# Two spectral transforms and two attention layers on one core: rows normalised in pairs, two more coefficient buffers, a feature-axis group run weight by weight, and a second transform that begins earlier

## The chip, the core and the metric

The kernel runs on one core of one Trainium2 chip, in one launch. The metric is the device time in microseconds (us), here the median of three runs. A core has engines that each work through their own queue of instructions in order: PE (TensorE: matrix products, with a separate unit for loading weights), DVE (VectorE), ACT (ScalarE), POOL (GpSimd), and SP (SyncE), which here issues nearly all transfers between the chip's main memory and the working memory. Products land in eight accumulator banks that DVE and ACT read out.

## What is computed

```python
x = A_x                                   # 2048 rows of 512 features
x = x + A(layernorm(x))                   # spectral layer
x = x + B(layernorm(x))                   # attention layer
x = x + A(layernorm(x))
x = x + B(layernorm(x))

A(x): a = x @ hid_re.T; b = x @ hid_im.T                # 512 x 512
      return seq_re @ a - seq_im @ b                    # 2048 x 2048
B(x): q, k, v = x @ wq, x @ wk, x @ wv                  # 32 heads of 16
      for s in range(4):                                # segments of 512 rows
          a_dot = causal softmax(qs @ ks.T / 4) @ vs
          a_mem = (phi(qs) @ M) / (phi(qs) @ z + 1e-6)
          o     = g * a_mem + (1 - g) * a_dot
          M, z  = M + phi(ks).T @ vs, z + sum(phi(ks))
      return o @ wo
```

All products of the transforms and projections are in 32-bit precision, made of three products of split operands: each operand is split into a high part and a low part, and high by high, high by low and low by high are added (`matmul3`). A "triple" below is these three matrix products.

## The kernel before

**How the work is ordered.** The program is written as generators that are resumed at numbered slots: `place(order, gen, slots)` says at which slots the next piece of a generator is written down. On PE that order is kept as written. For the other engines and for the SP queue a scheduler orders the instructions; what it makes of them stands in the fences below. On every engine the order is fixed once the program is built: an instruction that waits holds up all behind it.

**First transform** (`place_spectral`, `direct=True`). The 16 row tiles of 128 rows are loaded (`load_rows`, four buffers with the tag `xt`), normalised one by one (`normalise`: `row_stats` for mean and variance on DVE, the power of -1/2 on POOL, `layernorm` for a correction step and the scaled row `xn` on DVE) and split into `xa` (high part on ACT, low part on POOL; both on DVE for row tile 0). The sequence axis is contracted first. `read_pairs(tcn, k)` loads the raw coefficients of step k into two buffers `craw`, one for the real and one for the imaginary part (cc = 0, 1), splits them into `chi` (ACT) and `clo` (DVE), and forms on DVE the four sums of coefficients that the second transform needs, in one of two halves of a ring `sring`, from where 1 MB goes to memory (`sum`). `contract(tcn)` is the product: per k 16 triples, which use row tiles k and k + 8. There are 4 x 8 such steps. Then the feature axis: `split_u` splits the result into `us`, and `hidden(tcn)` multiplies by the feature-axis weights `wdt` into banks `y`, one row tile after the other, 8 triples each; `finish` adds the old row (`xr`) and stores it to `mid`. The slot `end` is where `hidden(0)` begins; two triples stand in a slot for tcn = 0, three in later ones.

**Attention** (`place_attention`). `prep` normalises and transposes a row tile into `xT`; `proj` makes q and k (`pqk`), `values` makes v (`pvv`). The 32 units (segment, head group, half of the group) are ten slots apart. A unit is `stack` (two loads, `stkq` and `stkk`, which share buffers with `chi` and `clo`), `natural_max` (scores in banks `nat`, row maxima by DVE at line 560, then `mparts`), `max_rows` (a transpose `mT`, whose result is copied by a transfer into `stkq`), `softmax_values` (scores `sT`, ACT's exponentials `pT`, POOL's causal masks, and the product `pv_bank`) and `output`. `natural_max` of a unit is written 17 slots ahead of its softmax. The first unit begins `LEAD` = 70 slots after `end`.

**Second transform** (`direct=False`): the coefficients and the stored sums are read in blocks (`read_block`, ring `cring`, split into `chi` and `clo`), and `product` gives groups of six products into banks `m`. It begins at slot `a2`, three slots before the slots of the first attention layer's units end.

Of the kernel before, what the change touches and what calls it, by code (L numbers as in the profile page):

```python
# [61 lines left out]
def spectral_infini_kernel(  # L62
# [29 lines left out]
    half_neg = consts.tile([P, 1], F32, name="half_neg")  # L92
# [40 lines left out]
    def row_stats(xt, mv=None):  # L133
        st = sb.tile([P, 6], F32, name="st", bufs=2)
        V.bn_stats(st, xt)
        mv = sb.tile([P, 2], F32, name="mv", bufs=3) if mv is None else mv
        V.bn_aggr(mv, st)
        ve = sb.tile([P, 1], F32, name="ve", bufs=3)
        V.tensor_scalar_add(ve, mv[:, 1:2], EPS)  # L139
        r = sb.tile([P, 1], F32, name="r", bufs=3)  # L140
        G.tensor_tensor(out=r, in0=ve, in1=half_neg, op=ALU.pow)  # L141
        return mv, ve, r

    first_row = []
# [4 lines left out]
    def layernorm(xt, mv, ve, r, rr=None):  # L149
        t = sb.tile([P, 1], F32, name="rt", bufs=2)  # L150
        V.scalar_tensor_tensor(t, r, r, ve, op0=ALU.mult, op1=ALU.mult)
        V.tensor_scalar(t, t, -0.5, 1.5, op0=ALU.mult, op1=ALU.add)  # L152
        rr = sb.tile([P, 1], F32, name="rr", bufs=2) if rr is None else rr
        V.tensor_mul(rr, r, t)
# [32 lines left out]
    def place_spectral(x_in, x_out, t0, end, ln_at, direct):  # L187
# [5 lines left out]
        def normal(i, xt, out):  # L193
            V.tensor_scalar(
                out, xt, row_mv[:, i, 0:1], row_r[:, i : i + 1], op0=ALU.subtract, op1=ALU.mult
            )

        def normalise(i):
            leads = i == 0 and direct
            xt = load_rows(x_in[i])  # L200
            yield
            with behind_first(i in (1, HALF, HALF + 1)):
                ve, r = row_stats(xt, row_mv[:, i])[1:]
            yield
            xn = layernorm(xt, row_mv[:, i], ve, r, row_r[:, i : i + 1])
            if not direct and i < HALF:
                G.tensor_tensor(
                    out=xn[:, D // 2 :], in0=xn[:, : D // 2], in1=xn[:, D // 2 :], op=ALU.subtract
                )
            xa[i] = pair("xa", "w", 16)  # L210
            lo = split(xa[i][:, 0], xa[i][:, 1], xn, lo_engine=V if leads else G, hi_engine=V if leads else A)
            if leads:
                first_row.append(lo[1])
            yield

        def add_rows(k):
            xt = [load_rows(x_in[i]) for i in (k, k + HALF)]
            yield
            e, o = [sb.tile([P, D], F32, name="xn", bufs=2) for _ in xt]
            normal(k, xt[0], e)  # L220
            normal(k + HALF, xt[1], o)
# [47 lines left out]
        def read_pairs(tcn, k):  # L269
            raw = [pair("craw", "craw", 2, F32) for _ in range(2)]  # L270
# [13 lines left out]
            if not ring:  # L284
                ring.append(sb.tile([P, 2, 4, 512], F32, name="sring", tag="xT", bufs=1))
            t = ring[0][:, k % 2]
            (r0, r1), (i0, i1) = ([raw[cc][:, h] for h in range(2)] for cc in range(2))
            for j, p, q in (0, r0, i0), (1, i0, i1), (2, t[:, 0], i1), (3, t[:, 2], r1):
                V.tensor_tensor(out=t[:, j], in0=p, in1=q, op=ALU.add)
# [91 lines left out]
        for i in range(NT):  # L381
            t = ln_at(i)
            place(3, normalise(i), [t, t, t] if i == 0 and direct else [t - 8, t - 3, t])
# [675 lines left out]
```

## Time and profile before

| | |
|---|---|
| runs | 1930.12, 1926.91, 1924.51 us; median 1926.91 us |
| the profiled execution's own time | 1924.58 us |
| its span in the trace | 1922.9 us |
| PE busy | 1811.9 us (94%) |
| DVE, ACT, POOL busy | 1325.3, 1058.9, 523.2 us |
| read from and written to main memory | 192.95 and 100.66 MB |

The profile is of one execution. A row of a timeline gives start, duration, engine, line, operation and the tiles (out<-in); in brackets is the idle time before it and what ended that. A table of stretches gives the busy time of each engine in each, the clock that TensorE was granted (1.00 is full), the share of time in which the transfer engines were busy, and GB/s.

### The profile page before, as it was taken

To read this page: it belongs to the slowest core of one execution; us is meant where nothing else is said; L and a number is where in the kernel's file an instruction comes from. 1 tells how busy PE (TensorE), PEld (TensorE's weight loads), DVE (VectorE), ACT (ScalarE), POOL (GpSimd) and SP (SyncE) were. 2 spreads that over 40 slices of the span, in tenths; PEclk is the share of its full clock that TensorE was granted. 3 is DMA by queue.
4 is the path that set the end of the run, shared out by engine and by line. 5 is a ranking of instruction groups with operands and counts; after the bars stand their busy time and mean duration, and the time that the engine had idled before them with its cause. 6 is when DMAs were issued, how large, how long until landed. Compare 5 with 4: busy or idle time off the path is not lost. (4 is left out here: it accounts for less than half of the span.)

```text
span 1922.9 us, 32039 instructions
## 1 busy us (share of the span) xinstructions
PE 1811.9 (94%) x10336; PEld 1302.1 (68%) x10336; DVE 1325.3 (69%) x4164; ACT 1058.9 (55%) x2292; POOL 523.2 (27%) x862
## 2 busy tenths in 40 slices
PE   6899999999889999999879999999989999999998
PEld 5688888788546656665448888877865566666654
DVE  7744546544877887867857687676567778777674
ACT  2221213313578777777664455443327877777775
POOL 4300000001444344546431000000044434444442
PEclk9999999999999999999989999999999999999999
DMA  6565555545434433433436677553464434344331
GB/s 217 178 203 191 181 200 188 182 143 180 153 114 143 130 120 114 147 120 120 146 100 209 212 239 238 188 180 110 165 197 127 128 96 148 115 131 141 109 122 45
DMA packets 165657, 296.51 MB, mean 154 GB/s; under 512 B 17776, under 2 KB 66928, under 8 KB 165488
## 3 DMA queue, kind: packets, MB, share of 16 engines
q1 hardware_dynamic: 162224, 293.68, 46.5%
q8 instruction: 81, 1.33, 0.3%
q10 hardware_dynamic: 3264, 0.79, 0.2%
q14 instruction: 88, 0.72, 0.1%
HBM read 192.95 MB, written 100.66 MB: 153 GB/s over the span
## 5 line engine op out<-in xcount | busy, mean ns | idle before, releaser
L560 DVE CUSTOM_DVE_ANT_0 junk<-nat,mask 128x512 bf16<-128x512 f32 (+3 forms) x1024 | 495.8, 484 | 168.1 <-PE nat L87 149.3
L626 ACT ACTIVATE pT<-sT 128x512 f32<-128x512 f32 x640 | 369.7, 599 | 15.4 <-ACT sT L625 3.4
L87 PE MATMUL u<-chi,xa 128*128 128x512 f32 x1024 | 320.4, 394 | 13.2 <-DVE xa L97 12.2
L629 POOL TENSOR_SCALAR_AFFINE_SELECT pT<-pT 128x256 f32<-128x256 f32 (+1 forms) x448 | 198.5, 457 | 411.4 <-ACT pT L626 345.9
L87 PE MATMUL nat<-stkk,stkq 96*128 96x512 bf16 (+3 forms) x1024 | 247.0, 303 | 20.7 <-DVE mx L560 15.6
L87 PE MATMUL sT<-stkq,stkk 99*128 99x256 bf16 (+3 forms) x1024 | 248.9, 306 | 13.4 <-DVE mx L560 6.8
L141 POOL TENSOR_TENSOR r<-ve,half_neg 128x1 f32<-128x1 f32 x64 | 38.5, 605 | 755.2 <-DVE ve L139 752.6
L625 ACT ACTIVATE sT<-sT 128x256 f32<-128x256 f32 (+1 forms) x640 | 207.8, 335 | 47.5 <-PE sT L87 40.4
L87 PEld LDWEIGHTS u<-chi,xa 128*128 128x128 f32 x1024 | 195.1, 191 | 54.7 <-issue 12.1
L87 PE MATMUL u<-clo,xa 128*128 128x512 f32 x512 | 202.3, 395 | 11.3 <-DVE clo L101 8.9
L99 ACT ACTIVATE chi<-craw 128x1024 fp32r<-128x1024 f32 (+1 forms) x66 | 68.2, 1034 | 225.6 <-DMA craw<-in_ct 133.3
L87 PE MATMUL y<-wdt,us 128*128 128x512 f32 x768 | 181.8, 391 | 3.3 <-DVE wdt L101 2.2
L87 PEld LDWEIGHTS <-stkk 99*128 99x128 bf16 x1024 | 82.5, 99 | 139.8 <-issue 121.0
L87 PE MATMUL pv_bank<-pT,vt 128*17 128x128 f32 (+3 forms) x2048 | 165.3, 450 | 9.7 <-POOL pT L629 9.7
L87 PEld LDWEIGHTS y<-wdt,us 128*128 128x128 f32 x768 | 143.3, 188 | 34.3 <-DVE wdt L101 3.3
L101 DVE TENSOR_TENSOR clo<-craw,chi 128x1024 fp32r<-128x1024 f32 (+1 forms) x66 | 79.5, 1206 | 103.8 <-ACT chi L99 103.6
L87 PEld LDWEIGHTS <-stkq 96*128 96x128 bf16 x1024 | 94.9, 99 | 74.6 <-issue 34.9
L87 PE MATMUL po<-wo,oh 128*128 128x512 f32 x384 | 126.8, 446 | 8.0 <-DVE rt L152 2.7
L87 PE MATMUL pqk<-xT,wq 128*128 128x512 f32 x384 | 132.0, 453 | 0.7 <-DVE mx L560 0.5
L87 PEld LDWEIGHTS pv_bank<-pT,vt 128*17 128x17 f32 x2048 | 59.6, 99 | 103.9 <-issue 79.6
L87 PE MATMUL pvv<-wv,xT 128*128 128x512 f32 x384 | 127.6, 445 | 1.6 <-DVE mx L560 1.6
L87 PE MATMUL pqk<-xT,wk 128*128 128x512 f32 x384 | 124.7, 434 | 0.0
(135 smaller groups left out, 3064.9 us busy)
## 6 DMA issues: line engine op xcount, KB each, us to landing
sum<-sring SPq DMA_DIRECT2D x32, 1024.0 KB
cring<-sum SPq DMA_DIRECT2D x128, 256.0 KB
craw<-in_ct SPq DMA_DIRECT2D x62, 512.0 KB
stkq<-scrq SPq DMA_DIRECT2D x64, 384.0 KB
stkk<-scrk SPq DMA_DIRECT2D x64, 384.0 KB
cring<-in_ct SPq DMA_DIRECT2D x96, 256.0 KB
xt<-mid SPq DMA_DIRECT2D x64, 256.0 KB
mid<-xo SPq DMA_DIRECT2D x48, 256.0 KB
```

Of the source, the lines that this page charges most:

```text
L87: return tc.keep_in_program_order(op(*args, **kwargs))
L99: A.activation(hi, src, AF.Copy, scale=scale)
L101: lo_engine.tensor_tensor(out=lo, in0=src, in1=hi.bitcast(F32), op=ALU.subtract)
L141: G.tensor_tensor(out=r, in0=ve, in1=half_neg, op=ALU.pow)
L560: V.tensor_tensor_reduce(junk[:, :n], src, mask[:, 512 - n :], 1.0, 3e38, ALU.add, ALU.min, dst,)
L625: A.activation(blocks, blocks, AF.Relu)
L626: A.activation(dst, ps, AF.Exp, scale=-SCALE)
L629: G.affine_select(blocks, blocks, pattern=[[0, n] for n in blocks.shape[1:-1]] + [[1, P]], compare_op=ALU.is_ge, fill=0.0, base=0, channel ...
```

## The change

- Rows are normalised two at a time: statistics of both, then one addition, one power and one correction (now four DVE operations in place of three) on 128x2 values, then both scaled rows. In the first transform the pairs are rows k and k + 8 (row 0 and row 8 stay single); in the second, neighbours, at other slots than before; in attention, neighbours.
- Raw coefficients of odd k go into the first half of the ring; its other half is left for the sums. So there are four raw buffers in place of two and one buffer for the sums in place of two.
- The set-up of masks and gates moves from slot 60 to 200, behind the sums of (1, 0).
- In both transforms the last feature-axis group (tcn = 3) is run weight by weight over its four row tiles at once (`hidden_last`: eight groups of 12 products, two slots apart, four banks `y` held from first to last). Its second half of `us` takes buffers of another tag. `LEAD` falls from 70 to 64.
- The first two feature-axis weights are loaded at `end` - 7 in both transforms.
- The second transform begins seven slots earlier, at LB - 10 in place of LB - 3 (LB is the number of slots of a layer's units).

```diff
+    def row_stats(xts, mv):
+        n = len(xts)
+        for j, xt in enumerate(xts):
+            st = sb.tile([P, 6], F32, name="st", bufs=2)
+            V.bn_stats(st, xt)
+            V.bn_aggr(mv[:, j], st)
+        ve = sb.tile([P, 2], F32, name="ve", bufs=3)[:, :n]
+        V.tensor_scalar_add(ve, mv[:, :, 1], EPS)
+        r = sb.tile([P, 2], F32, name="r", bufs=3)[:, :n]
+        G.tensor_tensor(out=r, in0=ve, in1=half_neg[:, :n], op=ALU.pow)
+        return ve, r
+
+    def row_scale(rr, ve, r):
+        t = sb.tile([P, 2], F32, name="rt", bufs=2)[:, : rr.shape[1]]
+        V.tensor_tensor(out=t, in0=r, in1=r, op=ALU.mult)
+        V.tensor_tensor(out=t, in0=t, in1=ve, op=ALU.mult)
+        V.tensor_scalar(t, t, -0.5, 1.5, op0=ALU.mult, op1=ALU.add)
+        V.tensor_mul(rr, r, t)
...
         def read_pairs(tcn, k):
-            raw = [pair("craw", "craw", 2, F32) for _ in range(2)]
+            if not ring:
+                ring.append(sb.tile([P, 8, 512], F32, name="sring", tag="xT", bufs=1))
+            if k % 2 == 0:
+                raw = [pair("craw", "craw", 2, F32) for _ in range(2)]
+            else:
+                raw = [ring[0][:, 0:2], ring[0][:, 2:4]]
...
-            t = ring[0][:, k % 2]
+            t = ring[0][:, 4:]
...
-                us[tcn, tt, cc] = t = pair("us", "w", 16)
+                home = ("ut", 8) if (tcn, cc) == (TC - 1, 1) else ("w", 16)
+                us[tcn, tt, cc] = t = pair("us", *home)
...
+        def hidden_last(tcn):
+            ps = [bank("y") for _ in range(LT)]
+            xr = []
+            order = list(range(2, 2 * DT)) + [0, 1]
+            for k in order:
+                cc, d = k // DT, k % DT
+                if k == order[-3]:
+                    xr = [load_rows(x_in[tcn * LT + tt], "xr") for tt in range(LT)]
+                for tt in range(LT):
+                    ut = us[tcn, tt, cc]
+                    matmul3(
+                        ps[tt],
+                        lambda h: ut[:, h, d * P : (d + 1) * P],
+                        lambda h: wdt[cc, d][:, h, :],
+                        k == order[0],
+                        k == order[-1],
+                    )
+                if k != order[-1]:
+                    yield
+            for tt in range(LT):
+                finish(ps[tt], xr[tt], x_out, tcn * LT + tt)
+            yield
...
-                    place(3, read_pairs(tcn, k), [t + 8 * k - 10, t + 8 * k - 4, t + 8 * k - 1])
+                    place(3, read_pairs(tcn, k), [t + 8 * k - 12, t + 8 * k - 4, t + 8 * k + 3])
...
-            t = end - 1 + k if direct and k < 2 else end - 12 + 2 * k if k < 2 else end - 3 + (k - 2) // 2
+            t = end - 7 + k if k < 2 else end - 3 + (k - 2) // 2
...
+            else:
+                at = run_from(end + nh // 2 + 2 * nh // 3 + 1, 2 * DT, 2)
...
-    LB, LEAD = NSEG * NG * (HG // HU) * 10, 70
+    LB, LEAD = NSEG * NG * (HG // HU) * 10, 64
...
-    a2 = b1 + LB - 3
+    a2 = b1 + LB - 10
```

**Place 1, DVE at the start of the program.** `row_mv`, `rt`, `row_r` and `xn` belong to row tile 0, `sring` and `craw` to the sums of step 0. Before:

```order
L135 BN_STATS st<-xt 128x6
L137 BN_AGGR row_mv<-st 128x2
L139 TENSOR_SCALAR ve<-row_mv 128x1
L289 TENSOR_TENSOR sring<-craw 128x512 x2
L289 TENSOR_TENSOR sring<-sring,craw 128x512
L151 SCALAR_TENSOR_TENSOR rt<-r,ve 128x1
L289 TENSOR_TENSOR sring<-sring,craw 128x512
L152 TENSOR_SCALAR rt<-rt 128x1
L154 TENSOR_TENSOR row_r<-r,rt 128x1
L156 TENSOR_SCALAR xn<-xt,row_mv,row_r 128x512
```

The same place now:

```order
L137 BN_STATS st<-xt 128x6
L138 BN_AGGR row_mv<-st 128x2
L140 TENSOR_SCALAR ve<-row_mv 128x1
L147 TENSOR_TENSOR rt<-r 128x1
L148 TENSOR_TENSOR rt<-rt,ve 128x1
L149 TENSOR_SCALAR rt<-rt 128x1
L150 TENSOR_TENSOR row_r<-r,rt 128x1
L159 TENSOR_SCALAR xn<-xt,row_mv,row_r 128x512
L97 CAST xa<-xn 128x512
L97 TENSOR_TENSOR xa<-xn,xa 128x512
```

The four sums of step 0 have gone behind the four low parts `clo` of that step. On SP the load of row tile 8 now stands behind the four coefficient loads of step 0, and no longer ahead of them. Further on in the first transform DVE's row of the sums of step k + 1 stands between the two `clo` of step k; before, the two `clo` stood together between two rows of sums.

**Place 2, PE around the first scores of the first unit** (`nat`; `y` is the feature axis, `pvv` and `pqk` are projections). Before:

```order
L87 MATMUL y<-wdt,us 128x512 x9
L87 MATMUL pvv<-wv,xT 128x512 x12
L87 MATMUL pqk<-xT,wq 128x512 x3
L87 LDWEIGHTS stkq
L87 MATMUL nat<-stkk,stkq 128x512
L87 MATMUL pqk<-xT,wq 128x512 x3
L87 LDWEIGHTS stkq
L87 MATMUL nat<-stkk,stkq 128x128
```

The same place now:

```order
L87 MATMUL y<-wdt,us 128x512 x12
L87 LDWEIGHTS stkq
L87 MATMUL nat<-stkk,stkq 128x512
L87 MATMUL pqk<-xT,wq 128x512 x3
L87 LDWEIGHTS stkq
L87 MATMUL nat<-stkk,stkq 128x128
L87 LDWEIGHTS stkq
L87 MATMUL nat<-stkk,stkq 128x384
L87 MATMUL pqk<-xT,wq 128x512 x3
L87 MATMUL y<-wdt,us 128x512 x12
```

Three of the eight groups of 12 `y` stand among the first unit's scores, where there was none; everything of the attention layer stands 54 products earlier against the feature axis.

**Place 3, PE in the last two units of the first attention layer**, from the transpose `mT` of the last unit on (`sT` scores, `m` the second transform). Before:

```order
L87 MATMUL mT<-ident_b,mparts_75 80x128
L87 LDWEIGHTS stkk
L87 MATMUL sT<-stkq,stkk 128x512
...
L87 MATMUL sT<-stkq,stkk 128x256
L87 LDWEIGHTS stkk
L87 MATMUL sT<-stkq,stkk 128x256
L87 MATMUL pv_bank<-pT,vt_68 17x512 x4
```

The same place now:

```order
L87 MATMUL mT<-ident_b,mparts_75 80x128
...
L87 MATMUL sT<-stkq,stkk 128x256
L87 MATMUL m_10563<-chi,xa 128x512 x3
L87 MATMUL m_10564<-chi,xa 128x512 x3
L87 LDWEIGHTS stkk
L87 MATMUL sT<-stkq,stkk 128x256
L87 LDWEIGHTS stkk
L87 MATMUL sT<-stkq,stkk 128x256
L87 MATMUL m_10581<-clo,xa 128x512 x3
L87 MATMUL m_10582<-clo,xa 128x512 x3
L87 MATMUL pv_bank<-pT,vt_68 17x512 x4
```

Two groups of six `m` now stand ahead of the `pv_bank` run of the last unit but one, where none did, and twelve ahead of that of the last unit, where five did.

More of the change, by code (lines that the diff above doesn't have):

```diff
@@ L91, in spectral_infini_kernel @@
     T = SimpleNamespace(matmul=in_order(T, "matmul"), transpose=in_order(T, "transpose"))
[L92 removed]
+    half_neg = consts.tile([P, 2], F32, name="half_neg")
     G.memset(half_neg, -0.5)
@@ L131, in load_split, with normal @@
         yield
[L133 to L144, printed above, removed]
+    def row_stats(xts, mv):
[15 more added lines that the diff above has]
+        V.tensor_mul(rr, r, t)
+    first_row, later = [], []
     def behind_first(wanted):
         return tc.issue_after(first_row[0].ins) if wanted and len(slots_done) < 40 else nullcontext()
[L149 to L154, printed above, removed]
+    def normal(xt, mv, rr):
         xn = sb.tile([P, D], F32, name="xn", bufs=2)
@@ L191, in place_spectral, with normalise @@
         ring = []
[L193 to L200, printed above, removed]
+        def normalise(n):
+            leads = n[0] == 0 and direct
+            xt = [load_rows(x_in[i]) for i in n]
             yield
-            with behind_first(i in (1, HALF, HALF + 1)):
-                ve, r = row_stats(xt, row_mv[:, i])[1:]
+            some = slice(n[0], n[-1] + 1, max(1, n[-1] - n[0]))
+            with behind_first(direct and not leads):
+                ve, r = row_stats(xt, row_mv[:, some])
             yield
[L205 to L213, printed above, removed]
+            row_scale(row_r[:, some], ve, r)
+            for i, src in zip(n, xt):
+                xn = normal(src, row_mv[:, i], row_r[:, i : i + 1])
+                if not direct and i < HALF:
+                    G.tensor_tensor(
+                        out=xn[:, D // 2 :], in0=xn[:, : D // 2], in1=xn[:, D // 2 :], op=ALU.subtract
+                    )
+                xa[i] = pair("xa", "w", 16)
+                engines = {"lo_engine": V, "hi_engine": V} if leads else {"lo_engine": G, "hi_engine": A}
+                lo = split(xa[i][:, 0], xa[i][:, 1], xn, **engines)
+                if leads:
+                    first_row.append(lo[1])
             yield
@@ L218, in add_rows @@
             yield
-            e, o = [sb.tile([P, D], F32, name="xn", bufs=2) for _ in xt]
-            normal(k, xt[0], e)
-            normal(k + HALF, xt[1], o)
+            e, o = (
+                normal(xt[n], row_mv[:, i], row_r[:, i : i + 1])
+                for n, i in enumerate((k, k + HALF))
+            )
             a, b = slice(0, D // 2), slice(D // 2, D)
@@ L283, in read_pairs @@
             yield
-            if not ring:
-                ring.append(sb.tile([P, 2, 4, 512], F32, name="sring", tag="xT", bufs=1))
-            t = ring[0][:, k % 2]
+            t = ring[0][:, 4:]
             (r0, r1), (i0, i1) = ([raw[cc][:, h] for h in range(2)] for cc in range(2))
             for j, p, q in (0, r0, i0), (1, i0, i1), (2, t[:, 0], i1), (3, t[:, 2], r1):
-                V.tensor_tensor(out=t[:, j], in0=p, in1=q, op=ALU.add)
+                with behind_first((tcn, k) == (0, 0)):
+                    summed = V.tensor_tensor(out=t[:, j], in0=p, in1=q, op=ALU.add)
+            if (tcn, k) == (1, 0):
+                later.append(summed)
             nc.sync.dma_start(sums[tcn, k].rearrange("j p s -> p j s"), t)
@@ L379, in hidden @@
                 yield
-        for i in range(NT):
-            t = ln_at(i)
-            place(3, normalise(i), [t, t, t] if i == 0 and direct else [t - 8, t - 3, t])
+        def hidden_last(tcn):
[14 more added lines that the diff above has]
+                        k == order[-1],
+                    )
+                if k != order[-1]:
[3 more added lines that the diff above has]
+            yield
+        for n, t in ln_at:
+            place(3, normalise(n), [t, t, t] if n[0] == 0 and direct else [t - 8, t - 3, t])
         if direct:
@@ L980, in setup @@
         nonlocal ident, ident_b, mask, same_head, gate
-        with tc.issue_after(first_row[0].ins):
+        with tc.issue_after(later[0].ins):
             ident = consts.tile([P, P], F32, name="ident")
```

51 lines of the change are left out of this document (30 added, 21 removed).

## The prediction

> **What bounds the kernel now.** I read the page's head first, then a table of the stages, then what PE waits for, and last the rows around its longest waits.
>
> ```profile
> span 1922.9 us, 32039 instructions
> PE 1811.9 (94%) x10336; PEld 1302.1 (68%) x10336; DVE 1325.3 (69%) x4164; ACT 1058.9 (55%) x2292; POOL 523.2 (27%) x862
> ```
>
> PE is busy for 94% of the span. No matrix product is added or removed, so what a change of order can give is PE's idle time, 111 us, and the time that PE spends at a lower clock. The stages say where these lie:
>
> ```profile
> 0.00:80.00 80.00, 55.44 (x214) 43.41 (x215) 64.93 (x152) 22.27 (x30) 37.74 (x48) 0.95 0.62 206
> 80.00:382.00 302.00, 301.65 (x1327) 249.36 (x1325) 155.05 (x210) 78.52 (x104) 0.00 (x0) 1.00 0.56 189
> 382.00:484.00 102.00, 100.20 (x448) 82.57 (x448) 49.22 (x110) 28.97 (x65) 13.99 (x14) 1.00 0.51 165
> 484.00:520.00 36.00, 30.22 (x156) 18.75 (x159) 30.36 (x130) 16.57 (x38) 14.65 (x21) 0.91 0.47 152
> 520.00:970.00 450.00, 418.00 (x2933) 261.93 (x2927) 352.54 (x1449) 335.56 (x796) 212.00 (x361) 0.97 0.39 126
> 970.00:1010.00 40.00, 30.68 (x199) 17.59 (x192) 20.61 (x55) 23.88 (x57) 12.53 (x24) 0.87 0.32 106
> 1010.00:1320.00 310.00, 308.23 (x1358) 253.45 (x1357) 228.75 (x402) 160.15 (x278) 7.90 (x8) 1.00 0.62 203
> 1320.00:1423.00 103.00, 101.84 (x457) 83.14 (x455) 53.77 (x122) 28.39 (x64) 13.99 (x14) 1.00 0.50 167
> 1423.00:1460.00 37.00, 31.24 (x180) 19.53 (x180) 31.26 (x130) 20.11 (x46) 18.08 (x24) 0.95 0.43 145
> 1460.00:1880.00 420.00, 400.57 (x2864) 252.63 (x2863) 322.90 (x1357) 322.00 (x766) 182.19 (x325) 0.98 0.39 123
> 1880.00:1922.90 42.90, 33.83 (x228) 19.77 (x227) 15.86 (x53) 22.48 (x55) 10.19 (x24) 0.95 0.15 51
> ```
>
> The columns are the stretch, its length, busy us of PE, PEld, DVE, ACT and POOL, the granted clock, the transfer engines' share and GB/s. PE is idle for 24.6 us in the first 80, for 5.8 us at each start of an attention layer (484 and 1423), for 9.3 us where the first attention layer ends (970), and for hardly any in the transforms. The change works on these four places. The attention bodies (32.0 and 19.4 us idle) and the tail it touches only through its paired rows. What PE waits for:
>
> ```profile
> PE u L87 <- DVE xa L97: 12.2, 1, 12.2
> PE mT L87 <- DVE mparts L583: 11.9, 3, 5.2
> PE pv_bank L87 <- POOL pT L629: 9.7, 6, 2.5
> PE u L87 <- DVE clo L101: 8.9, 3, 5.7
> ```
>
> **Term A, the first 80 us.** PE's first products and its two longest later stops, and DVE's rows ahead of them:
>
> ```profile
> 12.16 0.77 PE L87 MATMUL u<-chi,xa 128*128 128x512 f32 x1 [12.16 <-DVE xa L97]
> 13.99 0.79 PE L87 MATMUL u<-clo,xa 128*128 128x512 f32 x1 [1.06 <-DVE clo L101]
> 58.67 0.50 PE L87 MATMUL u<-clo,xa 128*128 128x512 f32 x1 [2.40 <-DVE rt L152]
> 76.29 0.79 PE L87 MATMUL u<-clo,xa 128*128 128x512 f32 x1 [5.71 <-DVE clo L101]
> ...
> 6.81 0.69 DVE L289 TENSOR_TENSOR sring<-craw 128x512 f32<-128x512 f32 x1 [2.36 <-DMA craw<-in_ct]
> 8.69 0.69 DVE L289 TENSOR_TENSOR sring<-craw 128x512 f32<-128x512 f32 x1 [1.19 <-DMA craw<-in_ct]
> 12.66 0.69 DVE L135 BATCH_NORM_STATS2 st<-xt 128x6 f32<-128x512 f32 x1
> 13.26 0.67 DVE L101 TENSOR_TENSOR clo<-craw,chi 128x512 fp32r<-128x512 f32 x1
> ```
>
> Row tile 0 waits on DVE behind the sums of step 0, which wait for coefficients until 8.69 us. With the sums behind it the row tile is done some 5 us earlier. PE's second product needs `clo`, and ahead of that `clo` stands the statistics row of row tile 8, whose load now follows four coefficient loads. The last of these four has landed by 8.69 now; I let the row tile land 0.3 us after it, and add 0.6 + 0.6 us from the starts 12.66, 13.26 and the clo's 0.67: 10.3 us for 13.99, a head start of 3.7.
>
> Then DVE is the bound up to the stop at 76.29. What DVE does for one row's correction, and how long it stands idle for POOL's power:
>
> ```profile
> L151 DVE SCALAR_TENSOR_TENSOR rt<-r,ve 128x1 f32<-128x1 f32 x16 | 7.6, 473 | 5.0 <-POOL r L141 4.8
> L154 DVE TENSOR_TENSOR row_r<-r,rt 128x1 f32<-128x1 f32 x16 | 4.4, 277 | 0.1
> L152 DVE TENSOR_SCALAR rt<-rt 128x1 f32<-128x1 f32 x16 | 2.2, 139 | 0.1
> L139 DVE TENSOR_SCALAR ve<-row_mv 128x1 f32<-128x1 f32 x16 | 2.1, 145 | 0.1
> ```
>
> (line, engine, operation, count, then busy us, mean ns, and idle before it; first 90 us.) Before: 16 x (473 + 277 + 139 + 145) ns = 16.5 us. Now nine groups of five operations; a 128x2 operation is not in the trace, and I price it as the 128x1 one, with 277 for each of three two-tensor operations: 9 x 1.115 = 10.0 us. That is 6.5 us less, and since rows overlap in DVE's pipeline (sums of durations exceed the stretch) I count two thirds, 4.3. The waits for the power, 4.8 us, fall by 7/16, 2.1. Against that, the single buffer for sums makes DVE wait for a write to land (landing times stand under rival 3), an estimate of 0.7 us in each of two steps where DVE's queue is full. So 3.7 + 4.3 + 2.1 less 1.4 is 8.7; I take A = 8.5 us. The ends are the head start alone, 3.7, and all of PE's idle time after 12.16 (24.6 - 12.2 = 12.4) with the head start, 16.1. The extra raw buffers are what lets the loads keep ahead; I give them no term of their own, since DVE and not a load ends the stops quoted. The moved set-up (five short DVE operations) I count at nothing: DVE is busy for 155 us of the 302 after 80.
>
> **Term B, the two starts of attention.** The columns are as in the timeline above:
>
> ```profile
> 500.53 0.33 PE L87 MATMUL mT<-ident_b,mparts 128*80 128x128 bf16 x1 [5.17 <-DVE mparts L583]
> 500.61 1.63 PE L87 MATMUL pvv<-wv,xT 128*128 128x512 f32 x3
> ```
>
> PE has done all it may do and waits for the first unit's maxima. Three groups of 12 `y` now stand inside this stretch: 36 products at 0.227 us (301.65 us for 1327 in the second stretch of the table, so 0.68 a triple) = 8.2 us, more than the 5.17. The group that follows the wait takes 1.63 us for three products, over twice 0.68, and the stretch's granted clock is 0.91: of its 36 us some 1.5 go to the clock besides. So 6.7 us could go at each start. What is late next: during the wait DVE did the statistics of the next segment's rows, and now that work, with two of the last four `finish` rows, comes into the units behind, where DVE is busy for 352.5 of 450 us. I let it take back 2.7: 4 us at each start, 8 in all. The ends for both are 0 and 13.4. The four banks held by `y` cost nothing in the sum: the scores get the PE work between them that lets DVE read banks out.
>
> The Trainium skill, in TensorE: Matmul & The Clock Gate (What's actually happening), says that the array falls to half its clock after an idle window of some 3.4 us and needs a busy one to come back. The trace agrees in that the 5.17 us wait is followed by half speed; by that rule an idle of 5.17 us would cost up to 1.7 us more, and the term would be 6.9 in place of 6.7 before the take-back.
>
> **Term C, the end of the first attention layer.**
>
> ```profile
> 981.05 1.04 PE L87 MATMUL sT<-stkq,stkk 99*128 99x256 bf16 x4 [1.62 <-DMA stkq<-mt]
> 986.31 4.12 PE L87 MATMUL pv_bank<-pT,vt 128*17 128x512 f32 x28 [2.39 <-POOL pT L629]
> ...
> 999.72 2.35 PE L87 MATMUL pv_bank<-pT,vt 128*17 128x512 f32 x32
> ...
> 984.14 0.69 DVE L135 BATCH_NORM_STATS2 st<-xt 128x6 f32<-128x512 f32 x1 [4.77 <-DMA xt<-mid]
> ...
> 985.33 0.55 POOL L141 TENSOR_TENSOR r<-ve,half_neg 128x1 f32<-128x1 f32 x1 [3.72 <-DVE ve L139]
> ```
>
> Read upward: PE's `pv_bank` waits for a mask on POOL, which stands behind a power, which waits for DVE, which waits 4.77 us for a row tile just written. In the new order that chain is still there: statistics directly behind the `finish` that stores their row. But two groups of `m` now stand in front of this `pv_bank` (2 x 6 x 0.227 = 2.7 us, against 2.39 idle), and PE stays warm: the 4.12 us run should come nearer to the 2.35 us of the next unit's 32, an estimate of 1.8 saved. The 1.62 us for the transfer stay, since both groups come behind it. Against these 4.2 us stand ACT and DVE, which must now split seven more blocks inside the last unit: I take C = 3.5. The ends are -1 (the blocks are late) and 6 (all of 1.62 too).
>
> **The small ones.** D: PE's 1.8 us idle at 382 is for the first feature-axis weights; their two buffers come free earlier, since odd steps no longer use `craw`: 1.3 us, ends 0 and 1.8. E: paired rows in both attention bodies and in the second transform spare DVE operations and halve its waits for the power. 51.4 us of PE idle lie in these bodies; I take 2, ends -2 and 5, because the same pairing puts two scaled rows in one piece before a maximum. The 128x2 power on POOL: nothing, POOL is 27% busy.
>
> **Sum.** A 8.5 + B 8 + C 3.5 + D 1.3 + E 2 = 23.3 us. The profiled execution took 1924.6 us (1922.9 and 1.7 around it), 2.3 below the median of the runs: 1924.6 - 23.3 = 1901.3, and as a median about 1903.
>
> **The rivals.**
>
> 1. *DVE stays the bound of the first 80 us*: only the head start comes, A = 3.7. For it: DVE is busy for 65 of the 80 us, and the sums of step k + 1 now stand between the two `clo` of step k, each behind the landing of the write before. Against: fewer operations and waits. Time 1903 + 4.8 = 1908.
> 2. *The starts and the end give it back*: B, C and E are nil, since attention is bound by DVE there (30.4 busy of 36 us at 484) and work taken out of a wait only makes the next maximum late. Gain 9.8; time 1926.9 - 9.8 = 1917. Both together: 1922, no change.
> 3. *Slower: the ring of sums paces the first transform.* The rows of one steady step, before:
>
> ```profile
> 217.43 9.96 SPq L274 DMA_DIRECT2D craw<-in_ct  x2
> ...
> 224.37 1.29 DVE L289 TENSOR_TENSOR sring<-craw 128x512 f32<-128x512 f32 x2 [1.49 <-DMA craw<-in_ct]
> ...
> 227.06 1.23 DVE L101 TENSOR_TENSOR clo<-craw,chi 128x1024 fp32r<-128x1024 f32 x1
> ```
>
> A step takes PE 16 triples x 0.68 = 10.9 us. In the new order a loop runs through `clo` (k, 1), the load of (k + 2, 1) into the freed buffer, the sums of k + 2 and `clo` (k + 1, 1): 6.9 us of landing (217.43 to 224.37), 2.7 of sums (224.37 to 227.06), 1.2 of clo and 0.3 of issue make 11.1. That is on the edge. If it landed at 8 us, the loop would be 12.2, and 28 steps would lose 1.3 us each, 36 us: 1903 + 36 = 1939. It decides from 7.6 us on (0.85 us x 28 is the gain of 23). Against it: the other part's load is now asked for a step sooner, so that only the 1 MB write and 0.5 MB stand in line, not 1.5 and 0.5 before it; the transfer engines are busy 0.56 of the time. I expect 5 to 6 us of landing.
>
> **How the numbers follow.** My forecast 0.55 (its own range 1894 to 1906), rival 1 0.18, rival 2 0.13, both 0.05, rival 3 0.09. The range reaches from the forecast with the upper ends of A and B half used (A + 4, B + 3, E + 2 and C + 2: 1892) to above rival 2: 1890 to 1920; it leaves out rival 3, both rivals together and the far ends. A measurement of this kernel can tell about 0.3%, 5.8 us, from no change. Faster: forecast, rivals 1 and 2, 0.86; same: 0.05; slower: 0.09.
>
> **What would show it.** A: first `clo` product near 10.3 us, the 12.4 us of later idle cut to half or less, the last `u` product near 374 in place of 382. B: no wait of `mT` for `mparts` at the first unit; the units after it a little longer. C: `m` rows between `sT` and `pv_bank`, the `pv_bank` run at 2.3 us. Rival 3: PE stops once a step beyond 100 us, each ended by a `clo`, and DVE waits for the write of `sum`. The forecast is wrong if the transform from 80 us on has idle PE, or if maxima make PE wait longer in the first units than they did.

## The result, and the profile after

The changed kernel took 1905.4 us (median of four runs, 1903.2 to 1912.8) for 1927.0 before: a ratio of 0.9894, 95% interval 0.9863 to 0.9924. A second set, taken beside three variants, gave 1906.2 us and 0.9885 (0.9871 to 0.9900); the experiments below are compared with that one. The forecast was 1903 us, in a range from 1890 to 1920, and the total is right. Three of its terms are not, and their errors cancel, which is luck; that is what the rest of this text is about.

The profile's head of the first execution, which was the slowest of its four, and some stages of its table of stretches (columns as before):

```profile
span 1911.1 us, 31877 instructions
PE 1809.7 (95%) x10336; PEld 1301.0 (68%) x10336; DVE 1311.1 (69%) x4073; ACT 1062.9 (56%) x2292; POOL 512.5 (27%) x831
...
0.00:80.00 80.00, 63.52 (x249) 50.13 (x250) 62.83 (x131) 23.94 (x32) 35.07 (x41) 0.96 0.66 224
80.00:379.00 299.00, 294.96 (x1294) 243.35 (x1293) 151.31 (x201) 72.76 (x91) 0.00 (x0) 0.99 0.55 187
480.00:540.00 60.00, 50.66 (x295) 31.71 (x294) 47.76 (x192) 35.96 (x80) 23.14 (x35) 0.91 0.52 161
```

The first 80 us have 8.1 us more of PE work than before, but the transform behind them now has 4 us of idle time, where it had 0.4. Around the start of attention PE is still idle for 9.3 of 60 us. Counts of stages don't say where time came from, since work was moved across their borders. Landmarks do: the same instruction looked up in both timelines. I take the first `y` of each transform, the transposes `mT` of the 32 units of each layer, and the last `m`. The table gives how many us earlier each comes than in the profile of before:

| landmark | changed, 1st profile | changed, 2nd | by rows | xr in `wd` | old slots | single prep | late m |
|---|---|---|---|---|---|---|---|
| first `y` | 2.8 | 3.9 | 5.7 | 5.5 | 3.7 | 4.4 | 3.6 |
| `mT` unit 3 | 0.1 | 4.0 | 7.7 | 7.1 | 1.6 | 3.6 | 0.9 |
| unit 5 | 6.6 | 10.5 | 14.3 | 13.7 | 8.1 | 5.4 | 7.5 |
| unit 10 | 6.7 | 10.5 | 14.3 | 13.7 | 8.2 | 5.3 | 7.5 |
| unit 15 | 4.6 | 9.0 | 13.2 | 13.1 | 6.2 | 5.8 | 5.1 |
| unit 20 | 4.8 | 9.2 | 13.3 | 13.1 | 6.2 | 5.9 | 5.2 |
| unit 29 | 12.8 | 16.3 | 23.2 | 23.1 | 6.5 | 13.9 | 14.1 |
| unit 31 | 11.7 | 15.6 | 22.2 | 22.5 | 6.3 | 13.2 | 13.3 |
| last `m` | 15.1 | 18.9 | 25.6 | 25.9 | 9.0 | 16.7 | 11.7 |
| 2nd layer, unit 3 | 9.8 | 13.1 | 23.2 | 22.7 | 2.6 | 12.6 | 4.9 |
| unit 5 | 16.0 | 19.3 | 29.5 | 28.9 | 8.7 | 13.0 | 11.1 |
| unit 15 | 14.6 | 16.9 | 28.0 | 27.8 | 6.3 | 12.9 | 8.8 |
| unit 31 | 14.4 | 16.6 | 27.9 | 27.5 | 6.4 | 12.5 | 8.8 |
| last product | 11.2 | 16.5 | 27.9 | 27.7 | 6.4 | 12.4 | 8.8 |

(The last five columns are experiments.) Read down the second: 3.9 us by the first `y`, nothing from there to unit 3, 6.5 from unit 3 to 5, 7.1 from unit 20 to 29, 3.3 at the end of the layer, then 5.8 lost at the start of the second layer, and 6.2 won at its units 3 to 5.

### The profile page after: what moved, and what is told of

Same layout as the page of the kernel before. It is cut to its first block, busy times and chain, and to the rows that moved or that the text cites. A ratio compares the mean times of both kernels' runs of the same rounds, so it can differ in the third digit from the quotient of the medians.

```text
span 1911.1 us, 31877 instructions
## 1 busy us (share of the span) xinstructions
PE 1809.7 (95%) x10336; PEld 1301.0 (68%) x10336; DVE 1311.1 (69%) x4073; ACT 1062.9 (56%) x2292; POOL 512.5 (27%) x831
## 5 line engine op out<-in xcount | busy, mean ns | idle before, releaser
L87 PE MATMUL nat<-stkk,stkq 96*128 96x512 bf16 (+3 forms) x1024 | 246.5, 302 | 20.8 <-DVE mx L603 12.4
L142 POOL TENSOR_TENSOR r<-ve,half_neg 128x2 f32<-128x2 f32 (+1 forms) x33 | 24.0, 728 | 696.5 <-DVE ve L140 692.9
L87 PE MATMUL pv_bank<-pT,vt 128*17 128x128 f32 (+3 forms) x2048 | 158.7, 440 | 1.7 <-POOL pT L672 1.6
L87 PEld LDWEIGHTS u<-clo,xa 128*128 128x128 f32 x512 | 97.7, 191 | 32.5 <-DVE clo L101 12.2
L99 ACT ACTIVATE clo<-cring 128x512 fp32r<-128x512 f32 x112 | 70.6, 631 | 69.1 <-DVE chi L101 37.9
```

What stands on the lines that cost most here:

```text
L87: return tc.keep_in_program_order(op(*args, **kwargs))
L99: A.activation(hi, src, AF.Copy, scale=scale)
L142: G.tensor_tensor(out=r, in0=ve, in1=half_neg[:, :n], op=ALU.pow)
```

## The experiments

Each ran five rounds. "Changed" is 0.9885 of the time before. The half-width of an interval is about 0.0015, 3 us.

### The changed kernel again

> The changed kernel as it is, for a second profile beside the variants. Its first profile came from the slowest of four executions (1912.8 us, the others 1903.2 to 1905.7), and there PE stands still for 3.3 us at 52.8, 1.7 at 55.0, 1.5 at 70.0 and 3.2 us at 107.3. Theory 1 (those 7 us lie in the first 120 us, where the order of landing of loads and of the 1 MB writes differs from run to run): median 1905, and if this profile's span is near 1903 the last product of the first contraction ends some 5 us earlier than the 378 us of the first profile. Theory 2 (the first 120 us are the same each time, the spread lies elsewhere): the same stops, and the last u product again at 378.

1906.2 us, ratio 0.9885. The stops in the first 120 us came again. In the eight profiles that share this code the first `y` leads by 2.8 to 5.7 us, 4.2 in the mean. So 3 us of spread do arise there, but the stops are always at the same places. Theory 2 holds for the places and theory 1 for some of the spread: the last stop (at 106 us) was 1.9 to 3.3 us long. Of the 5.2 us between the two profiles of the changed kernel at the last product, 1.2 arise before the first `y`, 2.8 between units 1 and 2 of the first layer, and 3.0 behind the last unit of the second; what lies between goes both ways and takes 1.6 back.

### The last group row by row

```diff
-            place(4, (hidden if tcn < TC - 1 else hidden_last)(tcn), at)
+            place(4, hidden(tcn), at)
...
-    LB, LEAD = NSEG * NG * (HG // HU) * 10, 64
+    LB, LEAD = NSEG * NG * (HG // HU) * 10, 70
```

(with the slots and the tag of `us` of the kernel before)

> The changed kernel with the last feature-axis group row by row again (hidden in place of hidden_last, LEAD 70, second half of us in its old tag) in both layers. Theory of the forecast (the two starts of attention are worth 4 us each): 1905 + 8 = 1913. Rival (by the landmarks of the two traces the first start is worth 2 and the second 1, since units 1 to 3 give back what the removed wait gave): 1908. A third (nothing is kept): 1905.

1896.3 us, 0.9836 (0.9822 to 0.9851): 9.9 us faster than the changed kernel. All three expectations were wrong: this part of the change costs time. The run undoes three things at once (the weight order, `LEAD` and the tag of `us`); the next two take them apart. The timelines show the transposes of units 0 to 3, first of the changed kernel (first profile), then row by row:

```profile
492.15 0.25 PE L87 MATMUL mT<-ident_b,mparts 128*80 128x128 bf16 x1 [1.48 <-DVE mparts L626]
508.13 0.33 PE L87 MATMUL mT<-ident_b,mparts 128*80 128x128 bf16 x1 [2.93 <-DVE mparts L626]
...
538.60 0.22 PE L87 MATMUL mT<-ident_b,mparts 128*80 128x128 bf16 x1
```

```profile
493.14 0.33 PE L87 MATMUL mT<-ident_b,mparts 128*80 128x128 bf16 x1 [5.12 <-DVE mparts L624]
504.57 0.22 PE L87 MATMUL mT<-ident_b,mparts 128*80 128x128 bf16 x1
...
530.93 0.22 PE L87 MATMUL mT<-ident_b,mparts 128*80 128x128 bf16 x1
```

The wait of 5.17 us at the first unit did fall to 1.48, and by rows it is back at 5.12. But from unit 0 to unit 3 the changed kernel takes 46.5 us (43.7 in its second profile), by rows it takes 37.8, as before (38.1). The wait was cheap: during it DVE did work that had to be done at some time. In the changed kernel this work is done later, between the maxima of units 0 and 1, and PE waits there: behind the first transpose its waits for maxima, up to unit 3, are 5.5 to 6.0 us in the changed kernel for 1.1 before. The groups of DVE between these two transposes, in the changed kernel (second profile, 16.0 us) and then by rows (11.4 us):

```profile
L137 DVE BATCH_NORM_STATS2 st<-xt 128x6 f32<-128x512 f32 x4 | 2.7, 670 | 0.0
L164 DVE TENSOR_TENSOR xo<-y,xr 128x512 f32<-128x512 f32 x2 | 1.4, 688 | 0.8 <-DMA mid<-xo 0.8
L101 DVE TENSOR_TENSOR wo<-raw,wo 128x512 fp32r<-128x512 f32 x2 | 1.4, 685 | 0.0
```

```profile
L137 DVE BATCH_NORM_STATS2 st<-xt 128x6 f32<-128x512 f32 x2 | 1.3, 674 | 0.0
```

Four statistics, two `finish` rows and two weight splits in place of two statistics: 4.2 us more of work and 0.8 of waiting.

### LEAD alone

```diff
-    LB, LEAD = NSEG * NG * (HG // HU) * 10, 64
+    LB, LEAD = NSEG * NG * (HG // HU) * 10, 70
```

> The changed kernel with one number changed: LEAD 70 in place of 64, so the last feature-axis group still runs weight by weight, but all its products stand ahead of the first unit's scores, as row by row they do. The run by rows took 1896.3 us for 1906.2. Theory 1 (the overlap costs: with products in the place of the 5 us wait, DVE gets its four finish rows and the maxima of units 0 to 2 in one stretch, 11.5 of 12 us busy at 496): 1897, the wait of 5 us for mparts is back, and units 1 to 3 follow 11 to 13 us apart in place of 14 to 17. Theory 2 (the weight order itself costs, by its four banks held to the end and the four finishes at once): 1905.

1906.2 us, 0.9897 (0.9885 to 0.9910): nothing gained. The wait is back (5.02 us), yet units 0 to 3 still take 43.3 us. So theory 1 falls: the overlap of products and scores is not what costs the 10 us. Something in the weight order itself puts DVE's work late.

### The old rows in other buffers

What do `finish` rows, statistics and `wo` have in common? `load_rows`: all are loaded through the four buffers `xt`. `hidden_last` loads four `xr` at once and frees them only at the four finishes.

```diff
-                    xr = [load_rows(x_in[tcn * LT + tt], "xr") for tt in range(LT)]
+                    old = [pair("xr2", "wd", 8, F32) for _ in range(LT // 2)]
+                    xr = [old[tt // 2][:, tt % 2] for tt in range(LT)]
+                    for tt in range(LT):
+                        nc.sync.dma_start(xr[tt], x_in[tcn * LT + tt])
```

> The changed kernel (0.9885 of the time before) with the four old rows xr of the last feature-axis group in two buffers of the tag wd, in place of all four buffers of the tag xt. LEAD stays 64 and the group still runs weight by weight. With LEAD 70 alone nothing was gained (0.9897), with the group by rows it was (0.9836). Theory 1 (held buffers: the four xr hold the buffers through which attention's rows and the weights wo are loaded, from their load to the finish rows, so DVE does these rows' statistics between the first and second unit's maxima in place of ahead of the first): 0.984 to 0.985, 8 us faster than the changed kernel, and units 1 to 3 follow 11 to 14 us apart. Theory 2 (the four finishes at once and the four banks held are what costs): 0.988 to 0.989.

1896.7 us, 0.9836 (0.9823 to 0.9848), 9.4 us faster than the changed kernel by the ratios, with LEAD 64 and the weight order kept. Theory 1 holds: held buffers cost what the whole part seemed to cost. Since `LEAD` and the tag of `us` stay as in the changed kernel, these are not the cause. The first two transposes, and DVE's groups between them:

```profile
491.63 0.33 PE L87 MATMUL mT<-ident_b,mparts 128*80 128x128 bf16 x1 [3.46 <-DVE mparts L629]
504.90 0.25 PE L87 MATMUL mT<-ident_b,mparts 128*80 128x128 bf16 x1 [0.79 <-DVE mparts L629]
```

```profile
L137 DVE BATCH_NORM_STATS2 st<-xt 128x6 f32<-128x512 f32 x3 | 2.1, 687 | 0.4 <-DMA xt<-mid 0.4
L164 DVE TENSOR_TENSOR xo<-y,xr 128x512 f32<-128x512 f32 x1 | 0.7, 691 | 0.0
```

The `wo` splits are gone from the stretch, and one `finish` and one statistics row with them: 13.3 us between the transposes, 40.0 from unit 0 to 3. The Trainium skill (Perfetto Trace Analysis, Optimization Strategy) says that a gap that keeps coming back can mean a lack of buffers for the next tile. The traces agree only in part: no wait of PE names a buffer, it names DVE's maxima. The shortage shows on the SP queue, where three loads of the next segment's rows are issued 14 us later in the changed kernel (second profile) than with `xr` in `wd`:

```profile
495.25 3.02 SPq L123 DMA_DIRECT2D xt<-mid  x3
```

```profile
481.02 1.68 SPq L123 DMA_DIRECT2D xt<-mid  x3
```

The statistics of these rows come behind their loads, so in the changed kernel they come behind the first unit's maxima.

With the buffers put right the weight order and `LEAD` 64 are still worth nothing: the group by rows took the same 0.9836.

### Rows of the second transform at the old slots

```diff
-        [((2 * j, 2 * j + 1), a2 + t) for j, t in enumerate((-40, -24, -8, 2, 14, 20, 32, 38))],
+        [((i,), a2 - 59 + 8 * i if i < HALF else a2 + 15 + 3 * (i - HALF)) for i in range(NT)],
```

> The changed kernel with the rows of the second transform normalised singly and at the slots of the kernel before; the products start as early as in the changed kernel. Theory of the forecast (pairing in the bodies is worth 2 us in all, of which this is a part): 1906. Rival from the traces (before, the transposes of maxima of units 21 to 27 of the first attention layer came 4.7 us, those of units 27 to 31 10 to 12 us later than now; the single rows at those slots held up DVE there): 1910 to 1911, with that 5 us back in units 21 to 27.

1915.9 us, 0.9934 (0.9916 to 0.9951): 9.7 us slower. The rival was right in mechanism and too small in size. From unit 20 to 31 its lead goes from 6.2 to 6.3 us, where the changed kernel's grows by 6.4. What PE waits for from 380 to 1010 us, changed (second profile) and then this run (sum, times, longest):

```profile
PE nat L87 <- DVE mx L603: 6.3, 12, 1.6
PE mT L87 <- DVE mparts L626: 5.7, 3, 2.9
```

```profile
PE nat L87 <- DVE mx L603: 10.6, 14, 1.6
PE mT L87 <- DVE mparts L626: 8.2, 3, 3.8
```

These two waits are 6.8 us longer, both for maxima. From unit 20 to 31 alone PE is idle for 21.4 us in place of 15.0, which is the lead that is missing. Rows of the second transform stand in DVE's queue among the maxima there in both kernels (eleven statistics in each, counted from unit 19 on); single and at the old slots they hold up the maxima more. The run undoes pairs and slots together; which of the two counts is not shown.

### Attention's rows single

```diff
-            for j in range(2):
-                t = b - (43, 51, 60, 60)[s] + 5 * j
-                place(2, prep(s, (2 * j, 2 * j + 1)), [t - 8, t - 5, t - 3, t, t, t + 2])
+            for i in range(LT):
+                t = b - (43, 51, 60, 60)[s] + (0, 2, 5, 7)[i]
+                place(2, prep(s, (i,)), [t - 8, t - 5, t - 3, t])
```

> The changed kernel with attention's own rows (prep) single again, at the slots of the kernel before; the transforms keep their pairs. Theory of the forecast (pairs spare DVE work: part of 2 us): 1906. Rival from the traces (the lead over the kernel before falls by 2.0 us from unit 11 to 15 of the first attention layer, and by 1.4 and 0.3 in the second, just where two scaled rows stand in one piece ahead of maxima): 1905 - 3.5 = 1901.5.

1909.3 us, 0.9898 (0.9881 to 0.9915): 3.1 us slower, within the intervals. The rival is wrong in the total. It saw one half: with single rows units 10 to 15 do keep their lead (5.3 to 5.8, where the changed kernel falls from 10.5 to 9.0). The other half is that units 3 to 5 gain 1.8 us in place of 6.5, and 0.4 for 6.2 in the second layer. The stop there, before, then in this run, then in the changed kernel (second profile), with POOL's power ahead of it in the first two:

```profile
549.14 4.01 PE L87 MATMUL pv_bank<-pT,vt 128*17 128x512 f32 x28 [2.53 <-POOL pT L629]
...
544.59 0.55 POOL L141 TENSOR_TENSOR r<-ve,half_neg 128x1 f32<-128x1 f32 x1 [2.63 <-DVE ve L139]
```

```profile
545.59 2.33 PE L87 MATMUL pv_bank<-pT,vt 128*17 128x512 f32 x28 [2.79 <-POOL pT L672]
...
540.78 0.55 POOL L142 TENSOR_TENSOR r<-ve,half_neg 128x1 f32<-128x1 f32 x1 [2.37 <-PE nat L87]
```

```profile
542.28 2.33 PE L87 MATMUL pv_bank<-pT,vt 128*17 128x512 f32 x28 [0.56 <-POOL pT L672]
```

It is the chain of term C at another place: a power on POOL that waits, masks behind it, `pv_bank` behind the masks. With pairs, at their slots, no power stands at this point of POOL's queue. What single rows lose here, 4.7 and 5.8 us of lead in the two layers, they win back in good part elsewhere, at units 10 to 15 above all, so that the whole run is only 3.1 us slower.

### The second transform's products late

```diff
-    a2 = b1 + LB - 10
+    a2 = b1 + LB - 3
```

(the rows at the same slots as in the changed kernel)

> The changed kernel with the second transform's products begun three slots before the end of the units in place of ten; the rows are normalised at the same slots as in the changed kernel. Theory of the forecast (3.5 us for the end of the first attention layer): 1909.5, and the end stops on pT, as before. Rival (the end is bound by DVE and POOL, so products moved there only change which wait is seen): 1906. By the landmarks of the traces (from the last maximum of the layer to the last m the changed kernel gains 3.3 to 3.4 us on the kernel before): 1909.5.

1909.7 us, 0.9919 (0.9903 to 0.9936), 6.5 us slower by the ratios, and the intervals don't touch. From the last maximum of the first layer to the last `m` the lead falls by 1.6 us, where the changed kernel's grows by 3.3: 4.9 us. The stop, changed (second profile) and then this run:

```profile
968.19 2.31 PE L87 MATMUL m<-clo,xa 128*128 128x512 f32 x6
...
971.89 2.33 PE L87 MATMUL pv_bank<-pT,vt 128*17 128x512 f32 x28 [0.42 <-POOL pT L672]
```

```profile
973.80 4.27 PE L87 MATMUL pv_bank<-pT,vt 128*17 128x512 f32 x28 [3.14 <-POOL pT L672]
```

The forecast's reading of this place holds: with `m` in front the wait falls from 3.14 to 0.42 us, and the run behind it takes 2.33 us in place of 4.27.

### Three on the first 120 us

The head start undone:

```diff
-                with behind_first((tcn, k) == (0, 0)):
+                with nullcontext():
                     summed = V.tensor_tensor(...)
```

> The changed kernel without the rule that the sums of step 0 come behind row tile 0. Theory of the forecast (the head start counts in full): first clo product back from 10 to near 13 or 14, and 1906 + 3.7 = 1910. Rival (DVE has the same work to do up to its last row at 72 us, so a later first product is caught up at PE's stops at 52 and 55): 1906.

1907.6 us, 0.9900 (0.9886 to 0.9914): 2.9 us slower by the ratios, not to be told from the changed kernel, and not from the forecast's theory either (3.7 us). The landmarks say more, and they lie between the two. The first `clo` product comes at 13.65 us in place of 9.57 to 9.96, the first `y` 0.4 and 1.6 us later than in the two profiles of the changed kernel, 1.8 later than in the mean of the eight. So half of the head start or more is lost again. PE's stops from the first `clo` product on make 8.8 us in place of 11.3 and 11.4. The stop of 4.7 to 4.9 us at 52 to 55 us (below), the same product counted from the start, shrinks to this:

```profile
57.90 0.50 PE L87 MATMUL u<-clo,xa 128*128 128x512 f32 x1 [3.76 <-DVE clo L101]
```

The stop at 70 us grows, from 1.5 and 1.9 us to 3.2, and those at 81 and 106 (3.7 to 4.1 us together) are gone. The rival has the mechanism, but not all of the places.

The first transform's rows single:

```diff
-        [((0,), a1 - 36), ((HALF,), a1 - 2)] + [((k, k + HALF), a1 - 6 + 8 * k) for k in range(1, HALF)],
+        [((i,), a1 - 6 + 8 * (i % HALF) + 4 * (i // HALF) - (30 if i == 0 else 0)) for i in range(NT)],
```

> The changed kernel with the rows of the first transform normalised singly at the slots of the kernel before; attention and the second transform keep their pairs. Theory of the forecast (pairs spare DVE 4.3 us of operations and 2.1 us of waits for the power where DVE is the bound): 6 us slower than the changed kernel, 0.9917, and the last u product near 383. Rival (a pair lengthens the chain: two scaled rows, two copies on ACT and two subtractions on POOL stand ahead of the next power, which is why PE stops for 4.8 us at 52 and 55 in every profile; what DVE is spared is spent waiting): 0.9885 within 1.5 us, with that stop smaller and others in its place.

1908.4 us, 0.9894 (0.9878 to 0.9911), and the first `y` at 378.3, not 383: the rival holds, and the forecast's 0.9917 lies outside the interval. PE's stop at 52 to 55 us is down to 0.3; its stops are other ones:

```profile
43.26 0.79 PE L87 MATMUL u<-clo,xa 128*128 128x512 f32 x1 [4.34 <-DVE clo L101]
72.96 0.79 PE L87 MATMUL u<-clo,xa 128*128 128x512 f32 x1 [4.43 <-DVE clo L101]
```

A second buffer for sums:

```diff
-            t = ring[0][:, 4:]
+            odd = k % 2 and tcn < 2
+            two = [pair("sums", "wd", 8, F32) for _ in range(2)] if odd else [ring[0][:, 4:6], ring[0][:, 6:]]
```

(the four sums go to `two`, and for odd k leave in two writes)

> The changed kernel with a second buffer for sums: for odd k of the first two column groups the sums go to two buffers of the tag wd, which is free until 260 us, and leave in two writes of 0.5 MB. DVE's five waits for a write between 73 and 114 us (22.3 us in all) should go. Theory 1 (rival 3 of the forecast in small: these waits cause PE's stops at 81 and 106, 0.5 to 3.3 us with 1 us of lower clock): 1906 less 3 to 4.5 = 1902. Theory 2 (DVE is behind anyway after 70 us, its own work sets these stops): 1906, with the stops ended by the same clo.

1901.9 us, 0.9872 (0.9858 to 0.9886): 2.5 us faster by the ratios, inside the intervals. The stop at 106 us is gone and DVE no longer waits for a write, but the stop at 81 us is longer (3.2 us for 0.5 and 0.8). The first `y` came at 374.2, 0.9 to 3.9 us earlier than in the eight profiles with one buffer. Theory 1 is favoured, but it is not settled.

### Together

By rows, with the second buffer for sums and single rows in segment 2 alone; and `xr` in `wd` with the second buffer:

> The changed kernel with three edits together: the last feature-axis group row by row with LEAD 70, the second buffer for sums, and attention's rows of segment 2 single again (the others in pairs). Apart, the first took 0.9836, the second 0.9872 (the changed kernel 0.9885), and single rows in all segments 0.9898, where units 11 to 15 kept 2 us of their lead in each of the first layers but unit 3 to 5 lost 6. Theory (they lie in different stretches, so they add): 0.9836 less 0.0015 less 0.001 to 0.002 = 0.980 to 0.981, about 1889 us. Rival (what one gives, the next start takes back): 0.983 to 0.984.

> Two edits that each gained: the old rows xr of the last feature-axis group in buffers of the tag wd (0.9836 of the time before), and the second buffer for sums (0.9872, the changed kernel 0.9885). They lie in different stretches, 460 to 560 and 60 to 120 us with their counterparts in the second layer. Theory 1 (they add): 0.982 to 0.983, 1893 to 1895 us. Theory 2 (what the first 120 us gain is lost again later, as in the run with three edits, whose lead of 30 us at unit 31 of the second layer fell to 27.6 by the end): 0.9836 to 0.984.

1896.9 us, 0.9841 (0.9823 to 0.9860), and 1896.5 us, 0.9840 (0.9824 to 0.9857). Neither adds anything that can be measured. In the first the lead was 30.6 us at unit 31 of the second layer and 27.6 at the last product; the second led by 2.0 us more than `xr` in `wd` at unit 5 and by 2.2 less at unit 23. In the first, units 10 to 15 lost 1.6 us of lead in the first layer and 1.9 in the second, though segment 2 had single rows. Why what is won early is lost there was not taken further.

The version to keep is the changed kernel with `xr` in the buffers `wd`: 0.9836 (0.9823 to 0.9848), faster than both kernels. The group by rows is as good.

## Why the prediction was right or wrong

The terms against the second profile, as changes of lead between landmarks:

| term | forecast | measured | where |
|---|---|---|---|
| A, first 80 us | 8.5 | 3.9 | first `y` |
| B, two starts | 8 | -7.9 | first `y` to unit 3, less D; last `m` to unit 3 |
| C, end of the first layer | 3.5 | 3.3 | unit 31 to last `m` |
| D, feature-axis weights | 1.3 | 2.2 | the waits of 1.2 and 1.0 us at the first `y` of the first layer are gone |
| E, pairs and their slots | 2 | 14.9 | units 3 to 31, and unit 3 to the end |
| sum (16.5 before rounding) | 23.3 | 16.4 | |

The two profiled executions differ by 17.0 us in span, the medians by 21.6 and 22.7: the profile of before lies 2.3 us under its median, the second one of the changed kernel 1.4 above. That the total came out right is luck: A and B fell 20.5 us short of the forecast, and E gave 12.9 us more. By the signs that the forecast itself named it is wrong twice: the transform behind 80 us has 4 us of idle PE, and maxima make PE wait longer behind the first unit than they did.

**A was mis-sized; it came out near rival 1's 3.7.** The head start was right (first `clo` product at 9.96 and 9.57 us, forecast 10.3), but the first `y` came at 378.1 and 376.9 us, where the last `u` was forecast for 374. The step "DVE is the bound, so fewer of its operations and waits are time won" failed. After its first `clo` product PE stops for 11.3 us, as before (11.3 too; the forecast's 12.4 counts the 1.06 us ahead of that product). So of what DVE was spared nothing reached PE in this kernel. Yet the head start alone is not the cause either: without it 2.3 us of the lead remain, as the experiment shows. In the changed kernel, first profile, with DVE's and POOL's rows that belong to them:

```profile
52.75 0.57 PE L87 MATMUL u<-chi,xa 128*128 128x512 f32 x1 [3.25 <-ACT chi L99]
55.01 0.80 PE L87 MATMUL u<-clo,xa 128*128 128x512 f32 x1 [1.69 <-DVE clo L101]
107.25 0.50 PE L87 MATMUL u<-clo,xa 128*128 128x512 f32 x1 [3.21 <-DVE clo L101]
...
49.67 0.16 DVE L147 TENSOR_TENSOR rt<-r 128x2 f32<-128x2 f32 x1 [1.91 <-POOL r L142]
...
46.44 2.55 POOL L101 TENSOR_TENSOR xa<-xn,xa 128x512 fp32r<-128x512 f32 x2 [5.55 <-ACT xa L99]
48.95 0.69 POOL L142 TENSOR_TENSOR r<-ve,half_neg 128x2 f32<-128x2 f32 x1
...
104.16 1.29 DVE L296 TENSOR_TENSOR sring<-craw 128x512 f32<-128x512 f32 x2 [6.04 <-DMA sum<-sring]
```

DVE was busy with the corrections for 13.3 us (16.3 before), where the forecast had 10.0: a 128x2 operation took 0.16 us alone, but 1.2 to 1.3 us where it met a subtraction on POOL. Two things took the place of what DVE was spared. First, a chain from pair to pair: scaled rows on DVE, both copies on ACT, both subtractions on POOL (2.55 us), only then the next power (48.95), for which DVE waits 1.91 us. The forecast took 7/16 off the waits for the power by counting powers; they rose instead, from 4.8 to 6.7 us, since in a pair each power stands behind twice the work. Second, rival 3 in small: DVE waits five times for the write of the sums (22.8 us in all), with `clo` behind it, up to 114 us. The forecast gave that 1.4 us; the stop at 107 alone is 3.2. That the waits cause this stop is likely, but the run with a second buffer does not settle it. Beyond it rival 3 did not come: no stop in any later step.

**B had the wrong sign.** The wait at the first unit went as foreseen. The step that failed is "I let it take back 2.7". I asked what DVE would do later, but not which buffers `hidden_last` holds while it runs; experiments by rows, LEAD 70 and `xr` in `wd` show that it is these for 9.4 us in all. But the gain of 4 us at each start does not come with the buffers either: with `xr` in `wd` PE still waits 3.46 us at the first unit, and at unit 3 its lead (7.1 us) is no larger than by rows (7.7). That is rival 2's account of the starts: work taken out of a wait only makes the next maximum late. By rows the first start costs nothing and the second 2.4 us, so a smaller part of the loss at the second start has another cause, which stays open. The 1.5 us for the clock failed too, as the last section shows.

**C was right,** by the chain named: the wait for the mask is down to 0.42 us, the slow run is gone, the wait for `stkq` is still there (1.76 us; 1.62 before).

**E was far too small.** I priced pairs as DVE operations spared. Their worth, with that of their slots, lies in queues: no power between masks at units 3 to 5 of both layers (6.5 and 6.2 us, of which 4.7 and 5.8 go with single rows), and rows of the second transform that hold up the maxima of units 20 to 31 less (6.3 us of lead there, 9.7 us in the whole run with the old slots). The loss at units 10 to 15 (1.5 and 2.5 us) goes with pairs in attention as a whole, but stays with single rows in segment 2 alone; whether two scaled rows ahead of a maximum cause it, as the forecast feared, is open. In the trace of before both stops could be seen, as `pv_bank` behind POOL's `pT` and `nat` behind `mx`. I had sorted them under "attention bodies" and did not ask what moved slots would do to them.

## What to carry to other kernels

When work is put into a wait of one engine, list what other engines did in that wait and which rotating buffers the new work holds: here four prefetched rows kept four shared buffers, and made a kernel 9 us slower, which two other buffers undid; the 5 us of the wait itself were not won even then. Price a batched small operation by its place in the in-order queues, not by its duration: a power that sat between masks cost 4.7 and 5.8 us of lead at two places, while sixteen corrections in place of nine made no difference that could be measured. And check a right total by landmarks before trusting its terms.

## What the runs showed of the hardware

A wait cut to 1.5 us did not save the granted clock. Stretches of 2 us at the first start of the changed kernel, second profile (columns as in the table of stages):

```profile
488.00:490.00 2.00, 0.65 (x4) 0.19 (x2) 1.96 (x6) 1.01 (x3) 1.16 (x1) 1.00 0.29 103
490.00:492.00 2.00, 1.02 (x5) 0.67 (x6) 1.86 (x10) 0.27 (x1) 0.00 (x0) 0.94 0.80 247
492.00:494.00 2.00, 2.00 (x8) 1.27 (x6) 1.15 (x6) 0.43 (x1) 0.00 (x0) 0.50 0.99 341
494.00:496.00 2.00, 2.00 (x9) 1.28 (x7) 1.66 (x6) 0.83 (x2) 0.00 (x0) 0.71 0.93 287
```

No wait here is longer than 1.48 us, but PE was busy for only 1.67 of 4 us, and then 4 us of full work ran at 0.50 and 0.71 of the clock. The rule of the Trainium skill (TensorE: Matmul & The Clock Gate, What's actually happening), which the forecast quoted, speaks of an idle window; this place shows that thin work can bring the fall too.

DVE and POOL slow each other. While both ran on two operands each, DVE's `clo` took 2.23 us where the next one takes 1.21, and POOL's two subtractions 4.27 where two earlier ones took 2.55 (the row stands above):

```profile
52.73 2.23 DVE L101 TENSOR_TENSOR clo<-sring,chi 128x1024 fp32r<-128x1024 f32 x1
57.76 1.21 DVE L101 TENSOR_TENSOR clo<-craw,chi 128x1024 fp32r<-128x1024 f32 x1
...
51.83 4.27 POOL L101 TENSOR_TENSOR xa<-xn,xa 128x512 fp32r<-128x512 f32 x2 [2.19 <-ACT xa L99]
```

The Trainium skill (SBUF — State Buffer, SBUF: two separate sides) says that these two engines share a pair of ports that one operation holds to its end, so that the other stands still; about 1 us lost on DVE and 1.7 on POOL fits that. The kernel before has such meetings too (a `clo` of 2.31 us at 26.87 us), so that pairs make more of them is not shown.
